# Beacon attention and a ReGLU FFN on one core: the first two batches loaded in 512 B runs and turned on TensorE, weights in 128-partition chunks, and FFN-only steps between the two batches

## The chip, the core and the metric

The kernel runs on one core of a Trainium2 chip. Its metric is the device time of one execution in microseconds (us), lower is better. The core has TensorE (PE in the profile; PEld is its weight load), VectorE (DVE), ScalarE (ACT) and GpSimd (POOL). SyncE (SP) issues most DMAs. SBUF is the on-chip memory, with 128 partitions; PSUM is the memory that matmuls write.

## The reference

The reference does causal attention with 16 extra "beacon" keys, and feeds the result to a gated FFN:

```python
# B, H, S, Nb, D = 8, 8, 576, 16, 64;  d_model = 512, d_ff = 1536
k_all = concat([beacon_k, k], axis=2);  v_all = concat([beacon_v, v], axis=2)
scores = q @ k_all.T / sqrt(D)            # beacons are always visible, the 576 tokens causally
a = exp(scores - max);  a /= a.sum(-1) + 1e-9
x = (a @ v_all) as [B*S, H*D]             # 4608 tokens x 512
out = (relu(x @ w_gate) * (x @ w_val)) @ w_out
```

All inputs and the output are float32. The kernel casts to bfloat16 on the way to TensorE and leaves out the subtraction of the maximum; a count at the end of whether all sums stayed in range guards a slower general path, which does not run with these inputs.

## The kernel before

**Data.** `xT` holds the attention output of all 4608 tokens in SBUF, features on partitions, as four blocks of 128 features (`KM` = 4). `wg`, `wv` and `wo` hold the three weights in bfloat16. A `Batch` owns `qT` and `kT` (transposed q and k) and `v`. Keys are counted with the beacons in front, in five tiles of 128 (the last has 80 rows).

**Attention.** Queries come in three chunks of 240, 256 and 80 columns (`CHUNKS`), heads in two groups of four. A `Unit` is up to 1024 columns of scores of one group: `qk` (L322) computes them on PE into one of two PSUM buffers, `exp` (L330) turns them into `e` on ACT, and L338 masks the diagonal block on POOL. When all units of a chunk and group are done, `Chunk.av` (L364) multiplies with `v` into `ab` and with ones into `os`. There is one buffer of each. `invert` (L372) takes the reciprocal of `os` on DVE, `scale` (L377) multiplies `ab` by it into `xT`, and `report` sends one row of each head's reciprocal to `rsum`.

**FFN.** An `Ffn` tile has 512 tokens. `up(nf)` computes 128 columns of the hidden layer: four gate matmuls (L399), a ReLU on ACT (L402), four value matmuls (L405) and a product on DVE into `hT` (L407). `down(ms)` computes 128 output rows with twelve matmuls (L412), copies them out of PSUM on ACT (L415) and leaves the store to SP for the next step (L417). All of these PSUM tiles come from `f_ps`, two buffers.

**Steps.** The whole order is written out by hand: 7 steps per batch, one batch after the other, and one more. A step issues the scores of two units, the products of the chunks that became due, and then FFN groups from a queue, as many as a credit allows: each step adds `QUOTA` = 4.5 (modelled us), and a group costs its columns x 8 / 2400, or 2.6 for a down. A stretch of tokens is put in the queue two steps after its last attention unit. Before, tile 0 comes as 0 to 240 and 240 to 512, each followed by the downs that it completes, and all other tiles come whole. What remains at the end runs after the last step.

**Loads.** `at(step, action)` hangs loads, casts and turns on steps; half of a step's actions run ahead of its FFN groups and half after them. Batch 0 is loaded at the start: k and q in two halves of 256 rows with two rows of one head per partition (`load_half`, runs of 512 B), cast, transposed on PE (L272) and copied to `kT` and `qT` (L275); the beacons and the last 64 rows go through `load_rows` and `turn_rows`. All other batches go through `fetch`: tile by tile `load` (runs of 256 B, L232), `cast` on POOL one step later (L247 for v, L250 for k and q), and a DMA transpose on SP (`turn`, L255), two steps after the load, for batch 1 one step after. Batch 1's fetch starts at step 1, batch 2's at step 7. Weights are issued on POOL (`load_w`, L298; `load_wo`, L303) in steps 0 to 5. Each engine works through its queue in order, SP's and POOL's among them, so a DMA or cast that waits holds up everything behind it on that queue.

Of the kernel before, what the change touches and what calls it, by code (L numbers as in the profile page):

```python
# [11 lines left out]
BF16 = mybir.dt.bfloat16  # L12
# [4 lines left out]
def general_path(tc, q, k, v, beacon_k, beacon_v, out, ident, wg, wv, wo):  # L17


    nc = tc.nc  # L20
    B, H, S, D = q.shape
    Nb = beacon_k.shape[2]
    P = 128
# [73 lines left out]
    with tc.tile_pool(name="gen_sb2", bufs=1) as sb, \  # L97
         tc.tile_pool(name="gen_ps2", bufs=1, space=bass.MemoryType.PSUM) as ps, \
         tc.For_i(0, B, 1) as i:
        x = sb.tile([P, KM, S], BF16, name="g_x")  # L100
        for hh in range(4):
            nc.sync.dma_start(
                x[hh * 32:(hh + 1) * 32],
                x_b[bass.ds(i, 1), hh * P:(hh + 1) * P].rearrange(
                    "o (k p) s -> p (o k) s", p=32))
        hT = sb.tile([P, NF, S], BF16, name="g_h")
        for nf in range(NF):
            for c in (0, HALF):
                gp = ps.tile([P, HALF], FP32, name="g_g")
                up = ps.tile([P, HALF], FP32, name="g_u")  # L110
                for dst, w in ((gp, wg), (up, wv)):
                    for ki in range(KM):
                        nc.tensor.matmul(dst, w[:, ki, nf * P:(nf + 1) * P], x[:, ki, c:c + HALF],
                                         start=(ki == 0), stop=(ki == KM - 1))
                gs = sb.tile([P, HALF], FP32, name="g_gs")
                nc.scalar.activation(gs, gp, AF.Relu)
                nc.vector.tensor_mul(hT[:, nf, c:c + HALF], gs, up)
        for t in range(NT):
            n = min(P, S - t * P)
            op = ps.tile([P, d_model], FP32, name="g_op")  # L120
            for nf in range(NF):
                nc.tensor.matmul(op[:n], hT[:, nf, t * P:t * P + n], wo[:, nf, :],
                                 start=(nf == 0), stop=(nf == NF - 1))
            ob = sb.tile([P, d_model], FP32, name="g_ob")
            nc.vector.tensor_copy(ob[:n], op[:n])
            nc.sync.dma_start(
                out_b[bass.ds(i, 1), t * P:t * P + n].rearrange("o s n -> (o s) n"), ob[:n])
# [26 lines left out]
def kernel(  # L154
# [52 lines left out]

    def by_group(a):
        return a.rearrange("p (x g d) -> p g x d", g=2, d=D)

    def grouped(a):
        return a.rearrange("p (g x d) -> p g x d", g=2, d=D)

    class Batch:
# [28 lines left out]
        def cast(self, x, t, copy):  # L243
            n = self.rows(x, t)
            raw = self.raw.pop((x, t))
            if x == "v":
                copy(self.v[:n, t], raw[:n])  # L247
            else:
                h = self.h[x, t] = half.tile([P, d_model], BF16, name="half")
                copy(grouped(h[:n]), by_group(raw[:n]))  # L250

# [11 lines left out]

        def turn_half(self, x, i, cast, move):
            raw = self.raw.pop((x, i, "half")).rearrange("p (h r d) -> p r h d", r=2, d=D)
            h = wide.tile([P, 2, d_model], BF16, name="hwide", bufs=2)
            for r in range(2):
                cast(grouped(h[:, r]), raw[:, r].rearrange("p (x g) d -> p g x d", g=2))
            ps = f_ps.tile([P, NP, 2, P], BF16, name="f")
            for r in range(2):  # L270
                for j in range(NP):
                    nc.tensor.transpose(ps[:, j, r], h[:, r, j * P:(j + 1) * P], ident)  # L272
            dst, c0 = (self.qT, 0) if x == "q" else (self.kT, Nb)
            c0 += i * 256
            move(dst[:, :, c0:c0 + 256].rearrange("a j (p r) -> a j p r", r=2),  # L275
                 ps.rearrange("a j r p -> a j p r"))

# [7 lines left out]
        def turn_rows(self, loaded, dst, cast, move):  # L285
            raw, n = loaded
            h = half.tile([P, d_model], BF16, name="half")
            cast(grouped(h[:n]), by_group(raw[:n]))  # L288
            ps = f_ps.tile([P, NP, n], BF16, name="f")
# [6 lines left out]
    def load_w(dst, src, n0, n1):  # L296
        for hh in (0, 2, 1, 3):
            nc.gpsimd.dma_start(  # L298
                dst[hh * C:(hh + 1) * C, :, n0:n1],
                src[hh * P:(hh + 1) * P, n0:n1].rearrange("(k p) n -> p k n", p=C))  # L300

# [41 lines left out]
    class Chunk:  # L343
# [6 lines left out]
        def av(self):  # L350
# [4 lines left out]
            for i, (kt, q0, n, _, _) in enumerate(order):  # L355
                e = self.batch.e.pop((self.g, self.ci, kt))
                kr = min(P, Stot - kt * P)
                for part in range(3):
                    for hh in range(4):
                        rows = slice(hh * C, (hh + 1) * C)  # L360
                        c0 = (2 * hh + self.g) * D + part * C
                        w = ones[:kr, :] if part == 2 else self.batch.v[:kr, kt, c0:c0 + C]
# [78 lines left out]
    STEPS = 7  # L441
    QUOTA = 4.5

    with tc.manual_schedule():
        first = Batch(0)
        batches = [first]
        dve, act, pool = nc.vector.tensor_copy, nc.scalar.copy, nc.gpsimd.tensor_copy
        wide_ctx = ExitStack()
        wide = wide_ctx.enter_context(tc.tile_pool(name="wide", bufs=4))

        beacon = first.load_rows(beacon_k[0])
        first.load_half("k", 0)
        first.load_half("q", 0)
        first.load("v", 0)
        first.load("v", 1)
        first.load_half("k", 1)
        first.load_half("q", 1)
        first.load("v", 2)
        first.load("v", 3)
        tail_k = first.load_rows(k[0, :, 512:])  # L460
        tail_q = first.load_rows(q[0, :, 512:])
        first.load("v", 4)

        first.turn_rows(beacon, first.kT[:, :, :Nb], dve, dve)
        first.turn_half("k", 0, dve, dve)
        first.turn_half("q", 0, act, act)
        first.cast("v", 0, pool)
        first.cast("v", 1, pool)

        w_actions = [lambda n=n, d=d, s=s: load_w(d, s, n, n + 384)  # L470
                     for n in range(0, d_ff, 384)
                     for d, s in ((wg, moe_w_gate), (wv, moe_w_val))]
        w_actions += [lambda i=i: load_wo(i, i + 6) for i in (0, 6)]

# [4 lines left out]

        at(0, lambda: first.turn_half("k", 1, pool, dve))  # L480
        at(0, lambda: first.turn_half("q", 1, pool, dve))
        at(0, w_actions[0])
        at(0, w_actions[1])
        at(1, lambda: first.cast("v", 2, pool))
        at(1, lambda: first.cast("v", 3, pool))
        at(1, lambda: first.turn_rows(tail_k, first.kT[:, :, 528:592], dve, dve))
        at(1, lambda: first.turn_rows(tail_q, first.qT[:, :, 512:576], dve, dve))
        at(1, lambda: first.cast("v", 4, pool))
        for j, w in enumerate(w_actions[2:]):
            at(1 + j // 2, w)  # L490

        def fetch(b, s0):
            at(s0, lambda: batches.append(Batch(b)))
            for j, u in enumerate(UNITS):
# [3 lines left out]
                if u[0] != "v":  # L498
                    at(s + (1 if b == 1 else 2), lambda u=u: batches[b].turn(*u))

        for b in range(1, B):
            fetch(b, STEPS * (b - 1) + (1 if b == 1 else 0))

        spans = [(0, 240), (240, 512)] + [(m, m + M_TILE) for m in range(M_TILE, n_tokens, M_TILE)]
        queue, have, credit = [], 0, 0.0
# [6 lines left out]

        for s in range(STEPS * B + 1):
            have = max([have] + [t for at_, t in ready.items() if at_ <= s])
            while spans and spans[0][1] <= have:
                t0, t1 = spans.pop(0)
                f = ffn_tiles[t0 // M_TILE]
                c0, c1 = t0 - f.m0, t1 - f.m0
                queue += f.groups(c0, c1, -(-c0 // P) if c0 == 0 else c0 // P, c1 // P)
            acts = later.pop(s, [])  # L520
            run_sp()
            b, i = divmod(s, STEPS)
            units = []
            if b < B:
                if i == 0:
                    batches[b].e = {}
                order = UNITS_BY_CHUNK if b == 0 else UNITS_BY_GROUP
                units = [Unit(batches[b], order[2 * i + x]) for x in range(2)]
# [5 lines left out]
            for c in chunks:  # L534
                c.av()
                c.invert()
            credit = min(credit + QUOTA, 2 * QUOTA)
            mine = []
# [9 lines left out]
            for j, (kind, _, run) in enumerate(mine):  # L548
# [3 lines left out]
                if j == 0:  # L552
                    for c in chunks:
                        c.scale()
                        later_sp.append(c.report)
                    chunks_done = True
                if second:
# [9 lines left out]
            for u in units:  # L567
                for g, ci, _, _ in u.parts:
                    left = [x for un in (order[2 * i + 2:]) for x in un if x[:2] == (g, ci)]
                    inside = [x for un in units for x in un.parts if x[0] == g and x[1] == ci]  # L570
                    if not left and inside and not any(c.g == g and c.ci == ci for c in due):
                        due.append(Chunk(batches[b], g, ci))
                        done = [x for un in order[2 * i + 2:] for x in un if x[1] == ci]
                        if not done:
                            ready[s + 2] = b * S + CHUNKS[ci][0] + CHUNKS[ci][1]
            if s == 3:
                wide_ctx.close()
        run_sp()
# [40 lines left out]
```

## Time and profile before

| | us |
|---|---|
| median of 9 runs | 442.18 |
| lowest and highest | 440.97 and 446.22 |
| profiled execution, its own time | 444.99 |
| its span in the profile | 443.3 |
| busy: PE, ACT, DVE, POOL | 389.6, 190.5, 174.9, 132.3 |
| PE busy in the first 26.6 us | 11.4 |
| PE busy from 26.6 to 66.6 us | 25.0 |
| PE busy from 66.6 to 116.9 us | 36.4 |
| PE busy from 116.9 to 158.5 us | 41.6 |

In the lines below, a group such as "PE L399" is TensorE's work of line 399. The words in brackets at the end give the idle time ahead of an instruction and what ended it. In the table of stretches the columns are the stretch, its length, the busy time of PE, PEld, DVE, ACT and POOL with their instruction counts, the granted PE clock (1.00 is full), the busy share of the DMA engines and the GB/s that they moved. GB/s counts the weights as bfloat16, half of what is read.

### The profile page before, as it was taken

The page shows a single profiled execution, that of the slowest core. Times are in us where ns is not written, and L with a number is a line of the kernel's source. Part 1 is how long each engine was busy: PE and PEld are TensorE (multiplying, and loading weights), DVE is VectorE, ACT ScalarE, POOL GpSimd, SP SyncE. Part 2 cuts the span into 40 slices and gives each one's busy share as a digit, 9 for nine tenths or more (in the row PEclk, how much of TensorE's full clock was granted, in tenths as well). Part 3 has the DMA queues.
Part 4 walks back from the last instruction along what each step waited for, and adds up shares of the span by engine and source line. Part 5 has one row for each costly group of instructions (what it writes and reads, how often), then busy time and mean ns, then how long its engine had stood idle before and what let it go on. Part 6 is the DMA issues. An engine that isn't in the chain of part 4 may idle for free.

```text
span 443.3 us, 10256 instructions
## 1 busy us (share of the span) xinstructions
PE 389.6 (88%) x4253; PEld 197.2 (44%) x4253; DVE 174.9 (39%) x232; ACT 190.5 (43%) x272; POOL 132.3 (30%) x242
## 2 busy tenths in 40 slices
PE   3487444799799999999999999999999999699994
PEld 2255312464445544454445444545544554244441
DVE  2544301342555354445453553455345425411320
ACT  3243204254465545546454555555546543123321
POOL 1995322534243324504151434133410200000000
PEclk9999756699999999999999999999999999889998
DMA  8989896695397358637843684557410020001002
GB/s 242 221 115 149 144 167 163 146 196 143 70 209 165 98 144 158 138 110 176 182 104 104 150 191 123 134 131 173 128 40 1 3 97 0 1 24 71 1 26 76
DMA packets 157397, 52.25 MB, mean 118 GB/s; under 512 B 142880, under 2 KB 152736, under 8 KB 157344
## 3 DMA queue, kind: packets, MB, share of 16 engines
q1 hardware_dynamic: 151168, 46.81, 45.2%
q0 software_dynamic: 6176, 4.72, 8.0%
q8 instruction: 35, 0.57, 0.6%
q14 instruction: 18, 0.15, 0.1%
HBM read 38.27 MB, written 9.44 MB: 108 GB/s over the span
## 4 chain that ended last, share of the span: by engine, by line
PE 80%; DMA 9%; DVE 4%; issue 2%; SPq 2%; POOL 2%; ACT 1%; DVEq 0%; ACTq 0%; POOLq 0%
PE f L405 23%; PE f L399 22%; PE f L412 21%; PE ab L364 6%; PE s L322 5%; DMA raw<-in_v_dram 5%; DMA raw<-in_q_dram 4%; PE os L364 2%; DVE r L372 2%; SPq L232 1%; POOL v L247 1%; DVE xT L377 1%; DVE half L288 1%; DVE hT L407 1%; POOL e L338 0%
## 5 line engine op out<-in xcount | busy, mean ns | idle before, releaser
L407 DVE TENSOR_TENSOR hT<-g,f 128x512 bf16<-128x512 f32 (+2 forms) x120 | 75.9, 632 | 131.9 <-PE f L405 128.9
L330 ACT ACTIVATE e<-s 128x1024 bf16<-128x1024 f32 (+2 forms) x112 | 105.3, 963 | 39.9 <-PE s L322 39.9
L399 PE MATMUL f<-xT,wg 128*128 128x512 bf16 (+2 forms) x480 | 118.5, 371 | 3.7 <-DMA wg<-in_moe_w_gate_dram 1.6
L405 PE MATMUL f<-xT,wv 128*128 128x512 bf16 (+2 forms) x480 | 116.5, 366 | 4.8 <-DMA wv<-in_moe_w_val_dram 3.0
L402 ACT ACTIVATE g<-f 128x512 f32<-128x512 f32 (+2 forms) x120 | 66.6, 555 | 117.6 <-PE f L399 116.3
L372 DVE RECIPROCAL r<-os 128x240 f32<-128x240 f32 (+2 forms) x48 | 65.2, 1358 | 107.8 <-PE os L364 82.2
L412 PE MATMUL f<-wo,hT 128*128 128x512 bf16 x432 | 99.7, 386 | 8.5 <-DMA wo<-in_moe_w_out_dram 8.5
L338 POOL TENSOR_SCALAR_AFFINE_SELECT e<-e 128x512 bf16<-128x512 bf16 (+2 forms) x80 | 46.7, 594 | 184.9 <-ACT e L330 178.0
L405 PEld LDWEIGHTS <-wv 128*128 128x128 bf16 x480 | 48.0, 100 | 65.3 <-issue 25.4
L399 PEld LDWEIGHTS <-wg 128*128 128x128 bf16 x480 | 45.6, 101 | 50.2 <-issue 7.1
L412 PEld LDWEIGHTS <-hT 128*128 128x128 bf16 x432 | 41.5, 99 | 58.9 <-DMA wo<-in_moe_w_out_dram 6.5
L415 ACT COPY ob<-f 128x512 f32<-128x512 f32 x36 | 21.1, 585 | 83.5 <-PE f L412 65.5
L250 POOL CAST half<-raw 128x512 bf16<-128x512 f32 (+1 forms) x70 | 41.4, 612 | 39.7 <-DMA raw<-in_k_dram 24.1
L364 PE MATMUL ab<-e,v 128*32 128x80 bf16 (+4 forms) x1408 | 42.7, 237 | 5.5 <-POOL e L338 3.9
L322 PE MATMUL s<-qT,kT 64*128 64x80 bf16 (+3 forms) x704 | 36.3, 239 | 9.8 <-DMA qT<-half 5.9
L322 PEld LDWEIGHTS <-kT 64*128 64x128 bf16 x704 | 22.1, 99 | 32.2 <-issue 24.8
L364 PE MATMUL os<-e,ones 128*32 128x80 bf16 (+4 forms) x704 | 35.0, 236 | 0.0
L364 PEld LDWEIGHTS <-v 128*32 128x32 bf16 (+1 forms) x1408 | 27.2, 99 | 15.0 <-issue 8.4
L377 DVE TENSOR_TENSOR xT<-ab,r 128x480 bf16<-128x480 f32 (+2 forms) x48 | 26.6, 553 | 0.7
L247 POOL CAST v<-raw 128x512 bf16<-128x512 f32 (+1 forms) x40 | 24.5, 619 | 7.6 <-DMA raw<-in_v_dram 7.5
L364 PEld LDWEIGHTS <-ones 128*32 128x32 bf16 (+1 forms) x704 | 19.5, 101 | 0.2
L298 POOL DMA_DIRECT2D wg<-in_moe_w_gate_dram x16 | 8.8, 558 | 0.0
(30 smaller groups left out, 38.6 us busy)
## 6 DMA issues: line engine op xcount, KB each, us to landing
out_dram<-ob SPq DMA_DIRECT2D x36, 256.0 KB
raw<-in_q_dram SPq DMA_DIRECT2D x28, 256.0 KB
raw<-in_v_dram SPq DMA_DIRECT2D x24, 256.0 KB
raw<-in_k_dram SPq DMA_DIRECT2D x21, 256.0 KB
raw<-in_v_dram SPq DMA_DIRECT2D x8, 224.0 KB
raw<-in_k_dram SPq DMA_DIRECT2D x7, 224.0 KB
wg<-in_moe_w_gate_dram POOLq DMA_DIRECT2D x16, 96.0 KB, 3.9
wv<-in_moe_w_val_dram POOLq DMA_DIRECT2D x16, 96.0 KB, 4.2
```

What stands on the lines that cost most here:

```text
L250: copy(grouped(h[:n]), by_group(raw[:n]))
L322: nc.tensor.matmul(self.s[:, a, c + j * n:c + (j + 1) * n], self.batch.kT[rows, 2 * g + j, kt * P:(kt + 1) * P], self.batch.qT[rows, 2 * g ...
L330: nc.scalar.activation(e[:, :k * 4 * n].rearrange("p (k a x) -> p a k x", k=k, a=2), self.s[:, :, :k * 2 * n].rearrange("p a (k x) -> p a ...
L338: nc.gpsimd.affine_select(out=cols[:, :, :m], in_=cols[:, :, :m], pattern=[[0, 4], [1, m]], compare_op=ALU.is_ge, fill=0.0, base=base, cha ...
L364: nc.tensor.matmul(o[:, q0 - cq0:q0 - cq0 + n], w, e[:kr, 2 * (hh % 2) + hh // 2], start=(i == 0 and part != 1), stop=(i == self.last), sk ...
L372: nc.vector.reciprocal(self.r[:, :n], self.os[:, :n])
L377: nc.vector.tensor_mul(xT[:, 2 * self.g:2 * self.g + 2, t0:t0 + n], self.ab[:, :, :n], self.r[:, :n].unsqueeze(1).to_broadcast([P, 2, n]))
L399: nc.tensor.matmul(g[:, :n], wg[:, ki, nf * P:(nf + 1) * P], x[:, ki], start=(ki == 0), stop=(ki == KM - 1))
L402: nc.scalar.activation(gs[:, :n], g[:, :n], AF.Relu)
L405: nc.tensor.matmul(u[:, :n], wv[:, ki, nf * P:(nf + 1) * P], x[:, ki], start=(ki == 0), stop=(ki == KM - 1))
L407: nc.vector.tensor_mul(self.h[:, nf, c0:c1], gs[:, :n], u[:, :n])
L412: nc.tensor.matmul(o, self.h[:, nf, ms * P:(ms + 1) * P], wo[:, nf, :], start=(nf == 0), stop=(nf == NF - 1))
```

## The change

The change has these parts:

- **Weights.** `load_w` no longer writes 32 partitions from four row blocks, but 128 partitions from two, with two neighbouring rows in one partition. This changes which feature lies in which partition of `xT`: v is stored with the even and odd columns of each head apart (the cast reads with a stride of two), and the head groups become heads 0 to 3 and 4 to 7, so q and k are cast without regrouping. The gate and value weights go out in three actions at steps 0, 1 and 2 (the last with 768 columns at once), `wo` at step 6.
- **Batch 0.** k's second half is cast on DVE instead of POOL. The move out of PSUM is cut in two, two head pairs each, which may go to different engines.
- **Batch 1** is loaded like batch 0, in halves at steps 5 and 6, and turned on PE at steps 8 to 11. It also takes batch 0's order of units.
- **Plan.** A list gives each step its batch and quota: batch 0 without FFN in its steps 0 to 4 and 4.5 in 5 and 6, then three steps of FFN alone, batch 1 with a quota of 1.75, and from batch 2 on 4.5 as before. A step number is thus three higher than before for the same place in batches 2 to 7; batch 2's fetch starts at step 10, batch 1's first step.
- **FFN stretches.** Tile 0 puts all its downs after the second stretch, and tile 1 is cut into 304 and 208 columns.

```diff
     def load_w(dst, src, n0, n1):
-        for hh in (0, 2, 1, 3):
+        for g in range(2):
             nc.gpsimd.dma_start(
-                dst[hh * C:(hh + 1) * C, :, n0:n1],
-                src[hh * P:(hh + 1) * P, n0:n1].rearrange("(k p) n -> p k n", p=C))
+                dst[:, 2 * g:2 * g + 2, n0:n1],
+                src[2 * g * P:2 * (g + 1) * P, n0:n1].rearrange("(p a) n -> p a n", a=2))
...
             if x == "v":
-                copy(self.v[:n, t], raw[:n])
+                copy(self.v[:n, t].rearrange("p (h a d) -> p h a d", a=2, d=C),
+                     raw[:n].rearrange("p (h d a) -> p h a d", a=2, d=C))
             else:
                 h = self.h[x, t] = half.tile([P, d_model], BF16, name="half")
-                copy(grouped(h[:n]), by_group(raw[:n]))
+                copy(h[:n], raw[:n])
...
-                        c0 = (2 * hh + self.g) * D + part * C
+                        c0 = (4 * self.g + hh) * D + part * C
...
+        def turn_half(self, x, i, moves):
+            h = self.h.pop((x, i, "half"))
             ps = f_ps.tile([P, NP, 2, P], BF16, name="f")
...
+            for g, move in enumerate(moves):
+                js = slice(2 * g, 2 * g + 2)
+                for r in range(2):
+                    for j in (2 * g, 2 * g + 1):
+                        nc.tensor.transpose(ps[:, j, r], h[:, r, j * P:(j + 1) * P], ident)
+                move(dst[:, js, c0:c0 + 256].rearrange("a j (p r) -> a j p r", r=2),
+                     ps[:, js].rearrange("a j r p -> a j p r"))
...
+    plan = ([(0, i, 4.5 if i > 4 else 0.0) for i in range(STEPS)]
+            + [(None, 0, 4.5)] * ALONE
+            + [(1, i, 1.75) for i in range(STEPS)]
+            + [(b, i, 4.5) for b in range(2, B) for i in range(STEPS)]
+            + [(None, 0, 4.5)])
...
+        at(0, lambda: first.cast_half("k", 1, dve))
+        at(0, lambda: first.turn_half("k", 1, (dve, dve)))
+        at(0, lambda: first.cast_half("q", 1, pool))
+        at(0, lambda: first.turn_half("q", 1, (dve, dve)))
+        at(0, lambda: load_both(0, 384))
...
+        at(1, lambda: load_both(384, 768))
+        at(2, lambda: first.cast("v", 4, pool))
+        at(2, lambda: load_both(768, 1536))
+        at(5, lambda: batches.update({1: Batch(1)}))
+        at(5, lambda: load_first(batches[1]))
+        at(6, lambda: load_rest(batches[1]))
+        at(6, lambda: load_wo(0, 6))
+        at(6, lambda: load_wo(6, 12))
...
+        def turn_second(x, i):
+            y = batches[1]
+            y.cast_half(x, i, pool)
+            y.turn_half(x, i, (dve, act))
...
-                    at(s + (1 if b == 1 else 2), lambda u=u: batches[b].turn(*u))
-
-        for b in range(1, B):
-            fetch(b, STEPS * (b - 1) + (1 if b == 1 else 0))
-
-        spans = [(0, 240), (240, 512)] + [(m, m + M_TILE) for m in range(M_TILE, n_tokens, M_TILE)]
+                    at(s + 2, lambda u=u: batches[b].turn(*u))
+
+        for b in range(2, B):
+            fetch(b, BASE[b] - STEPS)
+
+        spans = ([(0, 240), (240, 512), (512, 816), (816, 1024)]
+                 + [(m, m + M_TILE) for m in range(2 * M_TILE, n_tokens, M_TILE)])
```

## The prediction

> **What bounds the kernel now.** I read the page's slices first, then busy time in stretches cut where the picture changes, then TensorE's instructions in order of time.
>
> The page (share of the span; then tenths busy in 40 slices of 11.1 us):
>
> ```profile
> PE 389.6 (88%) x4253; PEld 197.2 (44%) x4253; DVE 174.9 (39%) x232; ACT 190.5 (43%) x272; POOL 132.3 (30%) x242
> PE   3487444799799999999999999999999999699994
> PEclk9999756699999999999999999999999999889998
> DMA  8989896695397358637843684557410020001002
> ```
>
> PE is full from the twelfth slice on. All that is lost lies in the first ten, where the granted clock falls too.
>
> Busy time in stretches:
>
> ```profile
> 26.60:66.60 40.00, 24.98 (x234) 15.54 (x232) 10.74 (x18) 9.46 (x18) 18.48 (x34) 0.80 1.12 153
> 66.60:116.90 50.30, 36.39 (x637) 23.61 (x636) 17.28 (x26) 21.68 (x33) 19.54 (x35) 0.86 0.70 150
> 116.90:158.50 41.60, 41.60 (x509) 20.44 (x498) 19.39 (x24) 21.60 (x30) 13.71 (x24) 1.00 0.59 138
> 158.50:200.00 41.50, 41.50 (x497) 20.40 (x498) 19.38 (x24) 21.95 (x31) 14.36 (x26) 1.00 0.63 144
> ```
>
> From 116.9 us a batch takes 41.5 us with PE never idle. Before that PE waits and runs at half clock. TensorE in order of time says for what:
>
> ```profile
> 43.38 0.96 PE L399 MATMUL f<-xT,wg 128*128 128x240 bf16 x4 [1.63 <-DMA wg<-in_moe_w_gate_dram]
> 47.38 0.96 PE L405 MATMUL f<-xT,wv 128*128 128x240 bf16 x4 [3.04 <-DMA wv<-in_moe_w_val_dram]
> 58.93 2.74 PE L412 MATMUL f<-wo,hT 128*128 128x512 bf16 x6 [6.20 <-DMA wo<-in_moe_w_out_dram]
> 63.97 2.72 PE L412 MATMUL f<-wo,hT 128*128 128x512 bf16 x6 [2.29 <-DMA wo<-in_moe_w_out_dram]
> 73.92 0.40 PE L322 MATMUL s<-qT,kT 64*128 64x128 bf16 x4 [4.77 <-DMA qT<-half]
> 80.29 0.59 PE L364 MATMUL ab<-e,v 128*32 128x240 bf16 x8 [3.89 <-POOL e L338]
> 115.28 0.29 PE L322 MATMUL s<-qT,kT 64*128 64x128 bf16 x4 [1.18 <-DMA qT<-half]
> 116.93 1.04 PE L399 MATMUL f<-xT,wg 128*128 128x512 bf16 x4
> ```
>
> Weights come late (16.2 us after 40 us with `wo`), then batch 1's transposed q and its mask. The bound is the start-up; afterwards it is TensorE.
>
> **Where the two kernels meet again.** Counting the FFN groups that the credit rule hands out: at the first step of batch 3 both kernels have finished tiles 0 and 1 whole (12 up and 4 down each) and hold the same 7 tiles and 5 batches, and both leave 7 up and 4 down of tile 7 and all of tile 8 for the end. In the trace of before that step's first FFN matmul starts at 158.41, so 443.30 - 158.41 = 284.9 us follow, the same in both. Only the time up to there can differ.
>
> **Batch 2's block (steps 17 to 23 after, 14 to 20 before).** Before: 158.41 - 116.93 = 41.5 us. After, tile 1 is split into 304 and 208 columns, and one 304 pair is done earlier. A gate and value pair took 1.85 us at 512 columns, 1.11 at 272 (matmuls starting at 91.52, 92.63, 93.74) and 1.13 at 240 (33.95, 35.09 and 36.22 on DVE's L407). That 240 costs as much as 272 shows a floor, so I put 304 at 1.21 and 208 at 1.05 (between 0.95 by columns and 1.13 by the floor). 11 x 1.21 + 12 x 1.05 = 25.9 against 12 x 1.85 = 22.2: +3.7. DVE's reciprocal (1.76) ahead of these short groups adds something like the 0.53 us stall at 99.05: +0.5. Block: 45.7 us. So the span after is t + 45.7 + 284.9, where t is the start of step 17's first FFN matmul; t = 112.7 breaks even.
>
> **Steps 0 to 4.** Until 26.6 us there is no FFN in either kernel. The cast of k's second half goes from POOL to DVE (0.38 each in place of 0.57), the q moves split in two, but q's second half still waits behind three masks and two casts on POOL; step 1's scores start near 16 us as now. Then quota 0 leaves the FFN out. ACT's exponentials (1.02 each) follow at once: step 3 in 26.3 to 28.3, step 4 to 30.4. The clock is still the slow one (240-column pairs took 1.60 at 29 to 32 us), so the four-tile value product of step 4, 1.33 us at 36.6, takes 2.66: 28.9 to 31.5. `ab` has one buffer, so the next one waits for reciprocal 1.76 and scale 0.68, and ends at 36.6. There the FFN starts, 10 us later than now; that is the price of attention alone.
>
> **Weights.** POOL issues 12 transfers of 256 rows and two of `wo` instead of 32 and two. A 128-row issue took 0.55, a 768-row one 0.84, so about 0.61 each: 7.3 us of POOL against 17.6. They go out at 15 to 29 us. At the 150 GB/s of the 25 to 35 us stretch, where only weights moved, 3.15 MB take 21 us: landed by 40; the FFN wants them from 36.6 to 48. SP holds batch 1's loads back behind the `rsum` report of step 4 (about 33.3), so they no longer share these microseconds. `wo` is issued at about 46, after step 6's mask, and is wanted at 71: 25 us for what took 14.5 last time. The weight waits of 16.2 us go, unless `wo` needs over 25 us.
>
> **Steps 5 to 9.** Twelve 240 pairs: two at 1.60, ten at 1.13, 14.5 us; scores and value products between them 1.8; the last reciprocal and scale 1.0: 53.9. Beacon and first k half turned on PE, with cast, 8 transposes (1.04 in the trace) and half a move (0.62): 2.6. Twelve 272 pairs 13.3, q's turn 1.7, one down 2.7, two turns 2.0. Sum: step 10 starts at 76. The 3.5 MB of batch 1 are issued at 34 to 44 and land by 58 at 150 GB/s, so the turns at 54 to 76 have their data.
>
> **Steps 10 to 16.** Nearest row: steps 11 to 13 of before, from 102.20 to 116.93, three steps and two downs in 14.7 us; without the downs (2 x 2.65) 3.1 each. Seven steps 21.9, three downs 8.0, one 304 pair 1.2: 31.1, so t = 107. With quota 1.75, PE is some 55% busy here. A rule of the Trainium skill speaks against this stage: "TensorE: Matmul & The Clock Gate", Part 1, halves the clock after an idle window of about 3.4 us and gives it back after as long a busy one. By that, with no gap of 3.4 us in my walk, nothing is added. The trace is stricter: at 43.38 a gap of 1.63 us was enough (four 240-column matmuls go from 0.57 to 0.96). By that row the first down and steps 11 and 12 run slow, +4 us; if all seven did, the 8 us of attention and 8 us of downs double, of which half falls into waits: +8. Between 0 and 8 I take +1, because steps 12 and 13 of before kept the clock with gaps of 0.5 to 1.2 us. t = 108.
>
> Beside this runs batch 2's fetch: casts on POOL, transposes on SP, both in order. SP's first transposes stand behind the output of step 11's down (about 87), then per tile 2.5 us of issuing, and load to cast 3.6 to 4.1 us (105.97 to 109.59, 90.81 to 94.94). I get tile 3's pair issued at 101.5 to 104 and landed by 106, just inside t. The strided cast of v is shown nowhere: 0.61 as the permuted k cast, up to 1.22 if the stride halves it; POOL is idle 70% of the time, so I take 0.61; at 1.22 five such casts put up to 3 us before the masks of this stage.
>
> Span 108 + 45.7 + 284.9 = 438.6 us. The profiled run of before took 444.99 with a span of 443.3, and the median of the runs is 442.18, 1.1 below the span. Predicted: **437.5 us**.
>
> **Rivals.** (1) *The fetch of batch 2 sets the end: slower.* In before batch 2's five pairs of transposes were issued from 87.83 to 117.3, 7.4 us per tile apart from the last. From 88 at that pace tile 3 starts at 110.2, lands at 113.9, and scores and values bring t to 115.4: median 444.9; at 8.5 a tile 448. For it: masks and casts share POOL's queue, and a mask behind a cast that waits for its load holds PE. Against it: the pace before was that of steps with 6.5 us of FFN in them. It decides from 6.5 us per tile, where t passes 112.7. (2) *Steps 10 to 16 do not wait at all*: clock kept, fetch early, t = 103: 432.5. For it the short ACT chain (2 us a step); against it the reciprocal and scale (2.4 us) with one `ab`. (3) *The half clock eats the gain*: +4 to +5, t near 112: 441.5.
>
> **How the numbers follow.** Likeliest case 0.46 (433 to 442), rival 1 0.27, rival 2 0.15, rival 3 0.12. Within 0.5% of 442.18 (440.0 to 444.4) is what a measurement of this kernel cannot tell from no change. Faster: 0.38 + 0.15 + 0.02 from cases likeliest, 2 and 3; same: 0.07 + 0.03 + 0.07; slower: 0.24 + 0.03 + 0.01. The range runs from rival 2 with a few us more gain to rival 1 at 9 us a tile: 429 to 450.
>
> **What would show it.** Right: no wait on wg, wv or wo; FFN starting near 36, scores of batch 1 near 76, t near 108, the block to batch 3 near 45.7 and 285 after it. Wrong: transposes of batch 2 ahead of step 17's scores, masks waiting behind casts, 12-matmul downs of 5 us in steps 10 to 16, or `wo` landing after 71.

## The result and the profile after

The changed kernel takes 446.73 us (median of 18 runs, 445.19 to 449.58); the kernel before, timed beside it, takes 442.70 (55 runs). The ratio is 1.0096, with a 95% interval of 1.0077 to 1.0114: slower by about 1%. Forecast was 437.5 and faster. The medians here and below are of all executions; the ratios leave out those in the slower of two states that executions on this chip show.

The page of the changed kernel, the same rows as of before:

```profile
PE 397.1 (89%) x4393; PEld 208.4 (47%) x4393; DVE 180.7 (41%) x258; ACT 193.6 (43%) x288; POOL 123.4 (28%) x220
PE   3478787776888999999999999999999999699994
PEclk9998999599899999999999999999999999989999
DMA  8999921567586246946663674368510010001002
```

The weak stretch has moved. Slices 4 to 7 are fuller than before, slices 8 to 13 are not full, and the clock falls in the eighth slice. PE has 7.5 us more busy time.

Busy time, cut at the step marks of the prediction (step 10; t, the first FFN matmul of step 17; about the first scores of batch 3):

```profile
26.60:76.79 50.19, 40.20 (x504) 28.39 (x504) 20.58 (x40) 17.25 (x35) 11.50 (x20) 0.93 0.75 149
76.79:114.23 37.44, 26.22 (x419) 14.24 (x417) 11.12 (x13) 15.64 (x20) 18.24 (x33) 0.80 0.64 147
114.23:161.00 46.77, 43.14 (x520) 27.76 (x518) 20.45 (x35) 21.63 (x40) 13.82 (x24) 0.98 0.54 124
```

In the first row PE is 80% busy at a clock of 0.93, more than in either row before 116.9 us of the old kernel. The second row, attention of batch 1 with few downs, leaves PE idle for 11 us at a mean clock of 0.80. In the third row, batch 2's block, PE is no longer full.

TensorE at the places the prediction named:

```profile
83.56 5.26 PE L412 MATMUL f<-wo,hT 128*128 128x512 bf16 x12
112.78 0.40 PE L322 MATMUL s<-qT,kT 64*128 64x128 bf16 x4 [3.95 <-DMA qT<-half]
114.23 1.20 PE L399 MATMUL f<-xT,wg 128*128 128x304 bf16 x4
117.41 0.68 PE L399 MATMUL f<-xT,wg 128*128 128x304 bf16 x4
118.72 0.68 PE L399 MATMUL f<-xT,wg 128*128 128x304 bf16 x4
161.97 1.04 PE L399 MATMUL f<-xT,wg 128*128 128x512 bf16 x4
```

Not one wait for `wg`, `wv` or `wo` is left. Step 11's down runs at half clock (5.26 us, where step 9's took 2.75). The scores of step 17 wait 3.95 us for batch 2's transposed q. Two pairs of 304 columns (a pair is a gate and a value group) start 1.31 us apart, and batch 3's first FFN matmul is at 161.97.

Against the prediction's sum, by span: t is 114.23 instead of 108 (+6.2), the block 47.7 instead of 45.7 (+2.0), the rest 283.7 instead of 284.9 (-1.2). Together that is the 7.1 us between 438.6 and 445.7.

SP's queue in the time that set t (an SPq line is the issue of a DMA, with the time that issuing took; lines in between are left out at "..."):

```profile
82.65 0.37 SPq L226 DMA_DIRECT2D raw<-in_v_dram  x1
89.47 0.36 SPq L417 DMA_DIRECT2D out_dram<-ob  x1
89.93 0.52 SPq L384 DMA_DIRECT2D rsum<-r  x1
90.55 1.79 SPq L250 DMA_TRANSPOSE kT<-half  x1
92.44 1.19 SPq L250 DMA_TRANSPOSE qT<-half  x1
93.69 0.57 SPq L226 DMA_DIRECT2D raw<-in_k_dram  x1
94.31 0.57 SPq L226 DMA_DIRECT2D raw<-in_q_dram  x1
94.93 0.85 SPq L226 DMA_DIRECT2D raw<-in_v_dram  x1
96.30 0.55 SPq L384 DMA_DIRECT2D rsum<-r  x1
96.96 1.24 SPq L250 DMA_TRANSPOSE kT<-half  x1
...
103.58 1.23 SPq L250 DMA_TRANSPOSE kT<-half  x1
...
108.99 1.24 SPq L250 DMA_TRANSPOSE kT<-half  x1
110.33 1.21 SPq L250 DMA_TRANSPOSE qT<-half  x1
```

SP stands from 83.0 to 89.5 in front of the store of step 11's down, although the casts that the first transposes need were done on POOL at 86.1. Then it issues almost without a pause: two transposes, three loads, a report or a store. That makes 6.15 us a tile from 90.55 to 108.99, and tile 3's q lands just before 112.8. The mask of batch 1's last chunk (the first of the two in the last line) was late by the same chain, as POOL shows:

```profile
109.00 0.61 POOL L245 CAST half<-raw 80x512 bf16<-80x512 f32 x1 [2.54 <-DMA raw<-in_k_dram]
110.34 0.61 POOL L245 CAST half<-raw 64x512 bf16<-64x512 f32 x1 [0.73 <-DMA raw<-in_q_dram]
111.48 1.00 POOL L338 TENSOR_SCALAR_AFFINE_SELECT e<-e 128x320 bf16<-128x320 bf16 x2
```

A third chain runs through the same queue. `r`, the reciprocal, has two buffers, so DVE's next reciprocal waits until an earlier one has been reported, and that report went out only at 108.34:

```profile
108.34 0.55 SPq L384 DMA_DIRECT2D rsum<-r  x1
110.79 0.66 DVE L372 RECIPROCAL r<-os 128x80 f32<-128x80 f32 x1 [7.00 <-DMA rsum<-r]
111.69 0.31 DVE L377 TENSOR_TENSOR xT<-ab,r 128x160 bf16<-128x160 f32 x1
```

Step 17's value products need that mask (done at 111.95) and `ab` free (112.00), and stand on PE behind the scores that need q (112.78). All three ends lie within 0.9 us, so an earlier q alone could have saved no more than about 0.8 us.

### The profile page after: what moved, and what is told of

Its sections match the earlier page's. It is cut to its first block, busy times and chain, and to the rows that moved or that the text cites. A ratio compares the mean times of both kernels' runs of the same rounds, so it can differ in the third digit from the quotient of the medians.

```text
span 445.7 us, 10542 instructions
## 1 busy us (share of the span) xinstructions
PE 397.1 (89%) x4393; PEld 208.4 (47%) x4393; DVE 180.7 (41%) x258; ACT 193.6 (43%) x288; POOL 123.4 (28%) x220
## 4 chain that ended last, share of the span: by engine, by line
PE 78%; DVE 6%; DMA 4%; POOL 3%; issue 3%; ACT 2%; SPq 1%; DVEq 0%; POOLq 0%; ACTq 0%
PE f L405 24%; PE f L412 20%; PE f L399 19%; PE ab L364 6%; PE s L322 5%; DVE hT L407 3%; PE os L364 3%; DMA raw<-in_q_dram 1%; PE f L274 1%; POOL e L338 1%; ACT e L330 1%; DVE r L372 1%; DMA wide<-in_k_dram 1%; POOL v L241 1%; DMA raw<-in_v_dram 1%
## 5 line engine op out<-in xcount | busy, mean ns | idle before, releaser
L407 DVE TENSOR_TENSOR hT<-g,f 128x512 bf16<-128x512 f32 (+4 forms) x132 | 77.7, 589 | 127.7 <-PE f L405 124.8
L405 PE MATMUL f<-xT,wv 128*128 128x512 bf16 (+4 forms) x528 | 117.1, 344 | 6.3 <-DVE hT L407 2.1
L402 ACT ACTIVATE g<-f 128x512 f32<-128x512 f32 (+4 forms) x132 | 68.6, 520 | 119.9 <-PE f L399 119.8
L399 PE MATMUL f<-xT,wg 128*128 128x512 bf16 (+4 forms) x528 | 118.3, 348 | 1.1 <-DVE cnt L435 0.7
L405 PEld LDWEIGHTS <-wv 128*128 128x128 bf16 x528 | 51.8, 99 | 64.6 <-issue 28.6
L399 PEld LDWEIGHTS <-wg 128*128 128x128 bf16 x528 | 49.4, 99 | 42.5 <-issue 3.1
L364 PE MATMUL ab<-e,v 128*32 128x80 bf16 (+4 forms) x1408 | 45.1, 243 | 5.2 <-DVE xT L377 3.8
L245 POOL CAST half<-raw 128x512 bf16<-128x512 f32 (+2 forms) x60 | 35.5, 612 | 14.7 <-DMA raw<-in_k_dram 11.1
L364 PE MATMUL os<-e,ones 128*32 128x80 bf16 (+4 forms) x704 | 36.6, 243 | 0.0
L274 PE MATMUL f<-ident,hwide 128*128 128x128 bf16 x64 | 8.1, 260 | 9.9 <-DVE kT L275 3.1
```

What stands on the lines that cost most here:

```text
L245: copy(h[:n], raw[:n])
L364: nc.tensor.matmul(o[:, q0 - cq0:q0 - cq0 + n], w, e[:kr, 2 * (hh % 2) + hh // 2], start=(i == 0 and part != 1), stop=(i == self.last), sk ...
L399: nc.tensor.matmul(g[:, :n], wg[:, ki, nf * P:(nf + 1) * P], x[:, ki], start=(ki == 0), stop=(ki == KM - 1))
L402: nc.scalar.activation(gs[:, :n], g[:, :n], AF.Relu)
L405: nc.tensor.matmul(u[:, :n], wv[:, ki, nf * P:(nf + 1) * P], x[:, ki], start=(ki == 0), stop=(ki == KM - 1))
L407: nc.vector.tensor_mul(self.h[:, nf, c0:c1], gs[:, :n], u[:, :n])
```

## Experiments

Theory A: SP's queue, above all its wait for the store, sets when batch 2's block (steps 17 to 23) starts, and the split of tile 1 makes that block longer. Rivals: the half clock of steps 10 to 12 (B), masks behind casts on POOL (C), the engines' own chain. "Beside before" is the ratio to the kernel before with its 95% interval; the changed kernel has 1.0096.

**Tile 1 whole.**

```diff
-        spans = ([(0, 240), (240, 512), (512, 816), (816, 1024)]
-                 + [(m, m + M_TILE) for m in range(2 * M_TILE, n_tokens, M_TILE)])
+        spans = ([(0, 240), (240, 512)]
+                 + [(m, m + M_TILE) for m in range(M_TILE, n_tokens, M_TILE)])
```

> The changed kernel with tile 1 of the FFN in one piece (512 columns) in place of 304 and 208; it still becomes available in step 16, so no step loses work. Theory A, the short groups cost PE time in batch 2's block: in the changed kernel a 304-column pair took 1.31 us (116.10 to 117.41) and a 208-column pair 1.05 (131.03, 132.02, 133.07), so 11 x 1.31 + 12 x 1.05 = 27.0 in the block against 11 x 1.85 = 20.4: 5.5 to 6.6 us faster than the changed kernel, about 440.7. Theory B, the block is paced by the waits of batch 2 and the short groups lie in them: within 1 us of the changed kernel, 446.

Measured: 439.75 us, 0.9928 (0.9901 to 0.9955) beside before: 7 us faster than the changed kernel, and faster than before. Busy time of this run up to and in batch 2's block:

```profile
76.79:115.48 38.69, 26.35 (x417) 14.52 (x422) 11.76 (x15) 15.91 (x20) 18.18 (x33) 0.80 0.68 144
115.48:155.76 40.28, 39.70 (x481) 19.79 (x488) 18.49 (x24) 21.14 (x29) 13.99 (x24) 0.98 0.70 143
```

The stretch before the block is as bad as it was (t = 115.48; a 512-column pair stands in it in place of a 304-column one), and the block, which now holds 11 pairs, falls from 47.7 to 40.3 us. So undoing the split is enough to turn the sign. Its mechanism is in the changed kernel's trace, around one 304-column pair:

```profile
118.21 0.68 PE L405 MATMUL f<-xT,wv 128*128 128x304 bf16 x4
118.99 0.47 DVE L407 TENSOR_TENSOR hT<-g,f 128x304 bf16<-128x304 f32 x1 [0.84 <-PE f L405]
119.52 0.55 PE L405 MATMUL f<-xT,wv 128*128 128x304 bf16 x3
```

`f` has two buffers, one in use for gate and one for value. The next value matmuls start 0.06 us after DVE has emptied the buffer of the last ones. So a pair lasts as long as value matmuls plus DVE product plus some 0.16 us of handing over: 0.68 + 0.47 + 0.16 = 1.31. The same sum gives 1.05 at 208 columns (0.52 + 0.37 + 0.16). 512 columns give 1.87 (1.02 + 0.69 + 0.16). PE alone would take some 1.06 at 304 (where no buffer is waited for, the next group starts after 0.53 us, 106.74 to 107.27), so cutting a tile pays the fixed part again: 1.31 + 1.05 = 2.36 against 1.87.

**Stores and reports of steps 10 to 17 on ACT's DMA queue.**

```diff
+    io = [nc.sync]
...
-            later_sp.append(lambda: nc.sync.dma_start(out[m:m + P, :], ob))
+            later_sp.append(lambda: io[0].dma_start(out[m:m + P, :], ob))
...
+            io[0] = nc.scalar if 10 <= s <= 17 else nc.sync
             run_sp()
```

(`report` in the same way.)

> The changed kernel with the stores and the reports of reciprocals of steps 10 to 17 issued on ACT's DMA queue instead of SP's. Theory A, SP's queue in order paces batch 2's fetch: the first transpose, at 90.55 behind the store of step 11's down, comes at about 87, and a tile takes about 5.3 us of SP in place of 6.15, so tile 3 is issued near 103 in place of 109.0 and step 17's first FFN matmul moves from 114.2 to 109 or 110: 4 to 5 us faster than the changed kernel, 442. Theory B, the half clock of steps 10 to 12 or the landing of the loads paces it: at most 1 us faster, 446.

Measured: 443.73 us, 1.0015 (0.9990 to 1.0040) beside before: 3 us faster than the changed kernel, where 4 to 5 were expected. SP and TensorE of this run:

```profile
82.22 1.32 SPq L250 DMA_TRANSPOSE kT<-half  x1
...
91.09 1.20 SPq L250 DMA_TRANSPOSE kT<-half  x1
...
96.40 1.20 SPq L250 DMA_TRANSPOSE kT<-half  x1
...
101.07 1.29 SPq L250 DMA_TRANSPOSE kT<-half  x1
```

```profile
74.66 0.60 PE L322 MATMUL s<-qT,kT 64*128 64x240 bf16 x12
108.57 0.40 PE L322 MATMUL s<-qT,kT 64*128 64x128 bf16 x8 [0.53 <-ACT e L330]
109.56 0.69 PE L399 MATMUL f<-xT,wg 128*128 128x304 bf16 x4
```

The first transpose comes 8.3 us earlier, tile 3 7.9 us earlier, the wait for q is gone and t is 109.56, where the expectation put it. Not all of this is the edit's doing: step 10 of this profile starts at 74.66, 2.1 us before that of the changed kernel (76.79), though the work ahead of it is the same. From step 10 to t it takes 34.9 us in place of 37.4. These 2.5 us fit the 3 us between the medians. Not as expected: the pace stayed at 6.3 us a tile, though SP now has pauses (87.2 to 91.1). So it is the start that was late; the pace is not SP's issuing alone. As the reports moved with the stores, the run frees the transposes and DVE's reciprocal together and does not tell the two apart.

**The same, with tile 4's casts and transposes a step later.**

```diff
+                late = int(b == 2 and u[1] == 4)
-                at(s + 1, lambda u=u: batches[b].cast(*u, pool))
+                at(s + 1 + late, lambda u=u: batches[b].cast(*u, pool))
...
-                    at(s + 2, lambda u=u: batches[b].turn(*u))
+                    at(s + 2 + late, lambda u=u: batches[b].turn(*u))
```

> As the run with ACT's queue, and also the casts and transposes of batch 2's tile 4 one step later, so that step 16's mask no longer stands behind them on POOL. Theory A (SP's queue): the same as that run, or 1 us less, since the mask stood at 111.5 only because its casts waited for loads that SP issued late. Theory C, the mask behind the casts is a bound of its own: 2 us or more faster than with ACT's queue alone.

Measured: 443.28 us, 0.9991 (0.9946 to 1.0035). The intervals do not separate it from the run before it, and they are wide enough to hide the 2 us of theory C. So C is not shown; beside SP's late loads, in the changed kernel itself, it was not tested alone.

**Downs in steps 10, 12 and 14.**

```diff
-            + [(1, i, 1.75) for i in range(STEPS)]
+            + [(1, i, q_) for i, q_ in enumerate((2.6, 0.0, 1.75, 1.75, 1.75, 1.75, 1.75))]
```

> The changed kernel with the quotas of batch 1's first two steps at 2.6 and 0 in place of 1.75 each: the downs move from steps 11, 13, 15 to 10, 12, 14, where PE waited. Theory B, the half clock in steps 10 to 12 is what made it late: the first down takes 2.7 us in place of 5.3 and its store leaves SP some 8 us earlier, step 17's first FFN matmul comes 3 to 5 us earlier, 442 to 443. Theory A (SP's queue alone): the first transpose comes earlier by the 3 us of its store's wait, but the pace of 6.15 us a tile remains: 2 to 3 us faster, 444. Neither, if SP is already behind by its loads: 446.

Measured: 442.22 us, 0.9960 (0.9920 to 0.9999): 4.5 us faster than the changed kernel, the size that theory B was given. TensorE and SP of this run:

```profile
76.00 2.55 PE L412 MATMUL f<-wo,hT 128*128 128x512 bf16 x11
84.65 3.69 PE L412 MATMUL f<-wo,hT 128*128 128x512 bf16 x10 [0.22 <-issue]
83.18 1.33 SPq L250 DMA_TRANSPOSE kT<-half  x1
101.81 1.25 SPq L250 DMA_TRANSPOSE kT<-half  x1
```

The slow clock is still there: ten matmuls of step 12's down take 3.69 us. But the down that the first transposes stood behind is now in step 10 and runs at full clock (11 matmuls in 2.55 us); its store is issued at 79.4, the transposes start at 83.18, and tile 3 is 7.2 us earlier. The edit does one thing more: with step 15 free of its down, three 304-column pairs run ahead of step 17 (12 gate matmuls there, 4 in the changed kernel), so two pairs, 2.6 us, leave the block. How much of the 4.5 us is the earlier store, how much the clock of one down and how much the two pairs, this run does not tell.

**Scores of steps 10 and 11 three times.** The output is unchanged; PE only repeats work.

```diff
-                u.qk()
+                u.qk(3 if s in (10, 11) else 1)
```

> The changed kernel with the score matmuls of steps 10 and 11 issued three times into the same PSUM tile, the same values, so that PE has work where it waited for the exponentials. It adds 2 x 24 score matmuls. If the half clock of the first down (5.26 us in place of 2.7) is a part of the delay: the down takes 2.7 to 3, its store leaves SP about 2 us earlier, and the kernel is 1 to 3 us faster, 444 to 445.5. If the clock does not depend on it, or the added work costs as much: 446.5 to 448.

Measured: 445.24 us, 1.0093 (1.0058 to 1.0129), against 1.0096 for the changed kernel.

```profile
81.48 4.12 PE L412 MATMUL f<-wo,hT 128*128 128x512 bf16 x12
109.32 0.40 PE L322 MATMUL s<-qT,kT 64*128 64x128 bf16 x4 [4.22 <-DMA qT<-half]
```

Step 11's down fell from 5.26 to 4.12 us only, and the wait for q stayed at 4.22. The median lies 1.5 us below that of the changed kernel, but the intervals do not separate the two. So with about half of the down's loss restored no gain is shown; what a full clock would be worth stays open.

**Batch 2's fetch from step 9.**

```diff
-            fetch(b, BASE[b] - STEPS)
+            fetch(b, BASE[b] - STEPS - (1 if b == 2 else 0))
```

> The changed kernel with batch 2's fetch started one step earlier, at step 9, and nothing else. Theory A, batch 2's fetch through SP's queue sets when its block starts: the first transposes now stand ahead of the store of step 11's down and are issued near 82 in place of 90.6, tile 3 at 6.15 us a tile near 101 in place of 109.0, and what is left is the chain of the engines, which in the changed kernel reached step 17's scores at 107.9: step 17's first FFN matmul near 109.5 in place of 114.2, 4 to 5 us faster, 442. Rival, the engines' own chain in steps 10 to 16 (half clock, one ab buffer) is the bound: at most 1 us faster.

Measured: 444.06 us, 1.0031 (1.0008 to 1.0055): 2.7 us faster than the changed kernel, less than expected. TensorE of this run:

```profile
83.45 0.41 PE L364 MATMUL ab<-e,v 128*32 128x128 bf16 x8 [1.80 <-POOL e L338]
111.80 0.69 PE L399 MATMUL f<-xT,wg 128*128 128x304 bf16 x4
```

No wait for the transposed q remains, and from step 10 to t it takes 33.5 us in place of 37.4. But a mask now stands behind the earlier casts (1.80 us), the wait of theory C, and the longer list of step 9 puts its two turns ahead of its FFN groups. In this profile step 10 starts at 78.30, 1.5 us later than in the changed kernel; whether the order of step 9 or the clock did that was not tested.

**FFN from step 3 on.**

```diff
-    plan = ([(0, i, 4.5 if i > 4 else 0.0) for i in range(STEPS)]
+    plan = ([(0, i, 4.5 if i > 2 else 0.0) for i in range(STEPS)]
```

> The changed kernel with the FFN quota of 4.5 already in batch 0's steps 3 and 4. The whole FFN work is the same; one down of tile 0 moves behind step 17's start. If attention alone in steps 3 and 4 wastes PE time (gaps of 0.69, 0.30 and 2.05 us and half clock from 25 to 33 us): 1 to 3 us faster, 444 to 445. If it buys the early loads of batch 1, which stand behind the reports of step 4 on SP: the second batch's turns come late, 2 us or more slower, 449 or more.

Measured: 446.13 us, 1.0090 (1.0046 to 1.0133): no change, which neither case had expected. Its first scores of step 10 start earlier (73.59), but the scores of step 17 wait 4.94 us for q, and then a down of tile 0 is still owed, which takes 5.06 us at 109.42. What the first steps save is lost there.

**The weight part alone, in the kernel before.** The diff is `load_w`, the cast of v, the head order and `c0` as in the change; all else is the kernel before.

> The kernel before with the weight part alone: 128-partition transfers, two in place of four per piece, with the order of features and heads that belongs to them; steps, loads, turns and the times of issue are those of before. My prediction put the weight waits (16.2 us at 43 to 64 us) down to late transfers. If the many 32-partition transfers made them late: 4 us or more faster, 438 or less. If the place of issue and the traffic of batch 1 made them late: wg and wv shrink by 1 to 3 us, wo stays, 440 to 442. If the strided cast of v costs: above 443.

Measured: 440.37 us, 0.9943 (0.9918 to 0.9968). TensorE of this run (its line 413 is line 412 of the kernel before):

```profile
53.79 2.74 PE L413 MATMUL f<-wo,hT 128*128 128x512 bf16 x6 [6.74 <-DMA wo<-in_moe_w_out_dram]
58.86 1.64 PE L413 MATMUL f<-wo,hT 128*128 128x512 bf16 x6 [2.33 <-DMA wo<-in_moe_w_out_dram]
```

The waits for `wg` and `wv` (4.7 us in the profile before) are gone altogether, those for `wo` stay at 9.1: the middle case, with the first half better than expected. The weight part is a gain, not the loss.

**The same with `wo` issued one step earlier.**

```diff
-            at(1 + j // 2, w)
+            at(1 + min(j, 5) // 2, w)
```

> The kernel before with the weight part, and wo issued in step 3, ahead of that step's casts on POOL, in place of step 4. With the weight part alone PE still waited 9.1 us for wo, which POOL issued at 45.9 behind a cast that waited for batch 1's k. If the place of issue was the cause: wo is issued near 34, the 9.1 us go, and of them 4 to 9 come off 440.4: 431 to 436. If batch 1's loads are held up in turn, or PE waits for batch 1's transposed q anyway (6.96 us at 70.1): 438 to 440.

Measured: 439.22 us, 0.9918 (0.9892 to 0.9945). `wo` went out at 33.3 and its waits shrank from 9.1 to 3.1 us, yet only about 1 us came off, which the intervals do not separate from nothing: batch 1's q is then waited for 6.81 us at 69.3, as with the weight part alone (6.96). In that start-up one wait covers the other.

**Together.** Tile 1 whole, downs in steps 10, 12 and 14, with and without ACT's queue, and with the earlier fetch:

> The changed kernel with three edits together: tile 1 whole, the downs in steps 10, 12 and 14, and the stores and reports of steps 10 to 17 on ACT's DMA queue. Theory A (the split costs PE time in batch 2's block, and SP's queue sets when that block starts): the first is worth 7.0 us alone, the second 4.5, the third 3.0; the last two remove the same wait of SP for a store, so together they give 4.5 to 6: 433.5 to 435.5. Rival, both are only faces of one wait: no better than the best of them alone, 439 to 440.

> The same without ACT's queue: tile 1 whole and the downs in steps 10, 12 and 14. Theory A: 446.7 - 7.0 - 4.5 = 435.2, 0 to 1.5 us slower than with ACT's queue. If reports and stores on SP still hold the transposes back, 437 or more.

> Tile 1 whole, the downs in steps 10, 12 and 14, and batch 2's fetch from step 9. In the run with the first two of these the wait for the transposed q at step 17 was down to 0.77 us. Theory A: the fetch is no longer the bound there, 0 to 2 us faster than that run, 435.5 to 437. If masks and casts on POOL come to stand in each other's way in steps 10 to 12: 439.

| | us | beside before |
|---|---|---|
| with ACT's queue | 437.43 | 0.9894 (0.9860 to 0.9927) |
| tile 1 whole, downs moved | 437.17 | 0.9863 (0.9788 to 0.9938, four runs) |
| that, fetch from step 9 | 438.42 | 0.9908 (0.9885 to 0.9930) |

All three beat both kernels by more than 0.5%, at about 1% below before. They gain 8.3 to 9.6 us on the changed kernel, not the 11.5 to 14.5 that the single gains add up to. The first was expected at 433.5 to 435.5; the other two lie nearer to their worse cases (437 or more, 439) than to the better ones. Between the three the intervals show no difference: once the down has moved, a gain from ACT's queue or the earlier fetch is not shown. They overlap with that of tile 1 whole alone (0.9901 to 0.9955) too, so for none of them is a gain beyond it shown. Part of what is missing goes after the block: from batch 3's first FFN matmul to the end the same work takes 285.8, 285.9 and 287.2 us in the three profiles, against 283.7 in the changed kernel. A wait of 1.74 us for DVE near 233 us is in each of them; the rest is not explained.

## Why the prediction was wrong

By span the miss of 7.1 us has four parts: 0.8 before step 10, 5.4 from step 10 to t, 2.0 in batch 2's block and -1.2 after it.

**Steps 0 to 9: right, in part by luck.** The start of the FFN was put at 36.6 and came at 34.6, as the clock had recovered for the last value product. The 272-column pairs then gave it back: at 1.22 us each instead of 1.11, and slow ones first. Step 10 was put at 76 and came at 76.8; with the same work ahead of it other runs show 74.6 to 77.8. The weights, at 0.71 us of POOL per 256-row issue instead of 0.61, were in time. The weight waits shown for before add up to 13.2 us, not to the 16.2 that the prediction names; its sum for t does not use that figure.

**Steps 10 to 16: the fetch beside them failed.** "I get tile 3's pair issued at 101.5 to 104 and landed by 106, just inside t" is the step. The first transposes were put at about 87 and came at 90.55, behind the store of a down at half clock. From there to tile 3 it gave three tiles some 14 us; they took 18.4. The two terms named for a tile, 2.5 us of issuing and 3.6 to 4.1 from load to cast, make 6.1 to 6.6 if one follows the other, and 6.15 was measured; the prediction let them overlap without a reason, and left out the loads, reports and stores that SP issues in between. That a report also holds a buffer that DVE needs was not in it at all. From step 10 to t:

| | us | wait for q at step 17 |
|---|---|---|
| predicted | 32 | none |
| changed kernel | 37.4 | 3.95 |
| stores and reports on ACT's queue | 34.9 | none |
| that, tile 4 a step later | 32.6 | 0.42 |
| fetch from step 9 | 33.5 | none |

So 2.5 to 4.8 of the 5.4 us go when SP's queue is relieved; the medians of these runs fell by 2.7 to 3.5. The rest is not assigned.

**Rival 1 took place**, in the path that it named, but not by its pace: it expected 7.4 us a tile from a start at 88, and it was 6.15 from 90.55, with t = 114.2. Its point of decision, t above 112.7, was passed by 1.5 us, which alone is little more than no change.

**The split was mis-sized.** The block was put at 45.7, 4.2 above before's 41.5; it took 47.7, 6.2 above. The pairs cost 4.8 (27.0 - 22.2) instead of 3.7, the rest 1.4 instead of 0.5: the first pair at half clock, DVE's reciprocal in front of short products. The 304-column pair was put at 1.21 because of a misread line. Its 1.11 us at 272 columns are the distance of gate groups that were still drawing ahead (the value group follows after 0.54, 0.65 and 0.76 us), which cannot last; the value groups of the same pairs in the kernel before stand 1.22 apart:

```profile
92.06 0.62 PE L405 MATMUL f<-xT,wv 128*128 128x272 bf16 x4
93.28 0.62 PE L405 MATMUL f<-xT,wv 128*128 128x272 bf16 x4
```

So 272 columns cost more than 240 (1.13), and there is no constant floor: the sum of value matmuls, DVE product and 0.16 us holds from 208 to 512 columns. With tile 1 whole the kernel is faster than before in spite of the fetch.

**The clock** was given +1 us between 0 and 8. Step 11's down alone took 2.6 us more, although PE's gaps since step 9's down were at most 1.17 us. That is less than the gap of 1.63 us after which the kernel before lost its clock, and no more than those with which it kept it (0.5 to 1.2 us). So neither the rule that the prediction quotes nor the length of a gap alone decides here. How much of this reached the end is not settled; the repeated scores show no gain clear of noise.

The forecast of the median missed 2.1 us more: before's median lay 1.1 us below the span of its profile, the changed kernel's 1.0 above.

## What to carry to other kernels

A list of transfers on an in-order queue is priced by every issue between two that matter, stores and small reports among them, and by the first wait at its head: a store that waits for a matmul group holds back the loads and transposes of the next batch, and a late report holds the buffer that it reads. Where a PSUM tile is written, read and written again through two buffers, a group costs its matmul plus its reader at any width; cutting it pays the fixed part again, so cut only where the earlier piece is also used. Here the first piece was available from step 13, but tile 0's downs took the quota up to step 15, and one 304-column pair ran ahead of the block. When a stage is freed, look at which transfer for the next stage is then late, before counting the gain.

## What the runs showed of the hardware

The strided cast of v cost next to nothing: 0.645 us on average against 0.619 for the contiguous one. POOL's issue of a weight transfer mostly took 0.71 us for 256 rows, between 0.55 for 128 and 0.84 for 768, but not on the line between them (0.61).

The order of work up to step 9 is the same in the changed kernel and in the runs e1, e2 and e8, and yet step 10 starts at 76.8, 77.3, 74.7 and 74.6. In the changed kernel the first 272-column groups of four matmuls after step 8's turn took 1.06 to 1.11 us, from 54.7 to 57.4; in e2 they took 0.62 from the start. So whether the clock falls at such a turn differed between executions of the same order of work, and a single profile carries 2 to 3 us of such differences.
